# Attention on one core: larger V pieces for pairs 56 and 57, and the last query chunk in six transfers

## The chip, the cores and the metric

The kernel runs on one core of a Trainium2 chip. The metric is device time in microseconds (us); lower is better. The core has TensorE (PE in the profile; its weight loads are PEld), VectorE (DVE), ScalarE (ACT), GpSimd (POOL) and SyncE (SP), and 16 DMA engines that all transfers share.

## What is computed

Grouped-query attention, 16 batches, 32 query heads over 8 key/value heads, 16 queries per head, 2048 keys, head size 128, all in bf16:

```python
B, Hq, Hkv, Sq, Sk, D = 16, 32, 8, 16, 2048, 128

def reference(q, k, v):
    rep = Hq // Hkv
    k = jnp.repeat(k, rep, axis=1)
    v = jnp.repeat(v, rep, axis=1)
    scores = jnp.einsum("bhqd,bhkd->bhqk", q, k) * D ** -0.5
    p = softmax(scores, axis=-1)
    return jnp.einsum("bhqk,bhkd->bhqd", p, v)
```

K and V are 64 MB each; queries and output are 2 MB each.

## The kernel before

**Tiling.** The 4 query heads that share a key/value head have 64 query rows together. The 128 (batch, key/value head) groups are taken two at a time: 64 pairs, numbered 0 to 63 (`NP = 64`). A pair has 1 MB of K and 1 MB of V. Its 128 query rows fill the 128 partitions.

**One pair.** SP loads K (`load_k`, L262) and, six steps later, V (`load_v`, L269). VectorE transposes K in 32x32 blocks (`kt`, L453, L461). TensorE makes the scores (`scores`, L318, L332). VectorE scales them, copies them to `Sneg` and takes the row minimum of the negated scores (L481). GpSimd exchanges the minima between the two halves of the partitions and makes the bias (`exchange`, L193, L208 to L216). ScalarE takes the exponential (`exp`, L520, L529). TensorE transposes the probabilities (`transposes`, L340, L350), ScalarE copies them to `PT` (`evict`, L535, L540), TensorE multiplies with V (`product`, L368), and ScalarE scales by the reciprocal of the row sum (`norm`, L545, L553).

**Two layouts of V.** For pairs below `P4 = NP - 8 = 56` each partition takes one piece of 8 KB of V, which belongs to one of the two groups of the pair; the product is then 64 matmuls, each with 64 rows of contraction (L402). For pairs from P4 on, each partition takes two pieces of 4 KB, one from each group; the product is 32 matmuls with 128 rows of contraction (L391). The layouts of the transposed K (L456), of `Sneg` (L475) and of the exponential's output (L524) follow the same test on P4.

**Queues.** All K, V and all query chunks but one are issued by SP in one order written out by hand (L293): at step t, K of pair t, then a query chunk when t = 4c - 3, then V of pair t - 6. V has four buffers, so its issue waits for the product four pairs earlier (L273); the last four V go to buffers of K (L131) and wait for a transpose of K instead (L271). V of pair 63 comes in two pieces (L284). The outputs of pairs 48 to 62 are held in `Oh` and stored by SP after all loads (L287); the other outputs are stored by ScalarE (L557).

**Queries.** A chunk is the 512 query rows of four pairs (`load_q`, L163): 128 partitions of 1 KB. There are 16 chunks, `NQC = 16`. GpSimd lays a chunk out in `Q4` in two halves (`lay`, L234, L160); before the first half it waits for the chunk's transfer. TensorE transposes them (L365), ScalarE copies them to `QT` (L515) and GpSimd takes each pair's part to `Qs` (L190).

**The end.** The engines run a prologue, a loop of eight steps, and the last pairs written out (`steps`, L120). TensorE's last four steps have an order of their own (L433 to L449): product 56 in `step(NP - 4, 0)`, then scores 62, six idle matmuls that only keep the clock up (`idle`, L409), product 57, scores 63, transposes 61, products 58 and 59, transposes 62, product 60, transposes 63, product 61, five idle matmuls, product 62, three idle matmuls, product 63. The products wait for their V (L371, L373, L389).

Of the kernel before, what the change touches and what calls it, by code (L numbers as in the profile page):

```python
# [16 lines left out]
NQ = 2  # L17
# [8 lines left out]
def bass_standalone__gqa_softmax__sampling_kernel(  # L26
# [18 lines left out]
    G = B * Hkv  # L45
    NP = G // 2
    assert NP % 8 == 0
    P4 = NP - 8
    PH = NP - 1 - sum(HELD)
    NQC = NP // 4  # L50
    scale = float(D) ** -0.5
# [11 lines left out]
    Qn = [sb(f"Qn{i}", [128, 4, 128], BF16) for i in range(NQ)]  # L63
# [24 lines left out]
    sem_q = [sem(f"sem_q{i}") for i in range(NQ)]  # L88
# [20 lines left out]
    qf = q.rearrange("b h s d -> (b h s) d")  # L109
# [6 lines left out]
    LO, HI, LOOP = PVLAG, PH + PVLAG, 8  # L116
    assert (HI - LO) % LOOP == 0 and HI <= P4 - 2


    def steps(eng, step, end):  # L120
        for p in range(LO):
            step(p, p)
        with eng.Fori(LO, HI, LOOP) as base:
            for i in range(LOOP):
                step(base + i, LO + i)
        for p in range(HI, end):
            step(p, p)
# [30 lines left out]
    def spread(eng, c, b):  # L158
        src = Qn[c % NQ][:, :, 64 * b:64 * b + 64]
        return eng.tensor_copy(Q4[:, :, b, :, :], src.unsqueeze(2).to_broadcast([128, 4, 4, 64]))  # L160


    def load_q(eng, c, s):  # L163
        src = qf[bass.ds(512 * c, 512), :].rearrange("(a j) d -> a (j d)", j=4)
        eng.dma_start(Qn[s][:, :, :].rearrange("a j d -> a (j d)"), src).then_inc(sem_q[s], 16)

    lo, hi = slice(0, 64), slice(64, 128)

    with nc.Block() as block:

        @block.gpsimd
        def _(gp):
            gp.memset(warm[:, :], 0.0).then_inc(sem_id, 1)
            gp.iota(iota_t[:, :], [[1, 128]], base=0, channel_multiplier=-1).then_inc(sem_id, 1)
            gp.wait_ge(sem_id, 2)
            gp.tensor_scalar(ident4[:, :], iota_t[:, :], 0.0, None, op0=ALU.is_equal).then_inc(sem_id, 1)


            def held(p):
                if not isinstance(p, int):  # L180
                    gp.nop(nofuse=True)

            def queries(p, i):
                if i % 4 == 0:
                    gp.wait_ge(sem_evq, p + 4)
                if i >= 2:
                    gp.wait_ge(sem_s, p - 1)
                held(p)
                x = i % 4
                gp.tensor_copy(Qs[i % 2][:, :, :], QT[i // 4 % 2][:, :, 128 * x:128 * (x + 1)].bitcast(BF16)).then_inc(sem_qs, 1)  # L190


            def exchange(p, i):  # L193
                known = isinstance(p, int)
                mins, sums = not known or p < NP, not known or p > 0
                x, s, t = slice(0 if mins else 2, 4 if sums else 2), i % NR, (i - 1) % NR
                if mins:
                    gp.wait_ge(sem_max, p + 1)
                if sums:
                    gp.wait_ge(sem_exp, p)  # L200

                gp.wait_ge(sem_qs, min(p + 2, NP) if known else p + 2)
                if known:
                    gp.wait_ge(sem_q4, 2 * laid(p))
                else:
                    gp.wait_ge(sem_q4, p - i + 2 * laid(i))
                held(p)
                gp.tensor_copy(oth[lo, s, x], own[hi, s, x]).then_inc(sem_x[0], 1)  # L208
                gp.wait_ge(sem_x[0], p + 1)
                held(p)  # L210
                gp.tensor_copy(oth[hi, s, x], own[lo, s, x]).then_inc(sem_x[1], 1)  # L211
                gp.wait_ge(sem_x[1], p + 1)
                held(p)
                if mins:
                    for h in range(2):
                        ins = gp.tensor_scalar(nbias[:, s, h:h + 1], own[:, s, h:h + 1], oth[:, s, h:h + 1], None, op0=ALU.min)  # L216
                    ins.then_inc(sem_b, 1)
                if sums:
                    for h, rows in enumerate((lo, hi)):
                        if h:  # L220
                            gp.wait_ge(sem_sum[0], p)
                            held(p)
                        gp.tensor_tensor(  # L223
                            rowsum[rows, t:t + 1], own[rows, s, 2 + h:3 + h], oth[rows, s, 2 + h:3 + h], op=ALU.add,
                        ).then_inc(sem_sum[h], 1)
                    gp.wait_ge(sem_sum[1], p)


            def laid(p):
                c, i = divmod(p, 4)  # L230
                return min(2 + c, NQC) + min(c + (i > 0), NQC - 1)


            def lay(c, b, base=0):  # L234
                if b == 0:
                    gp.wait_ge(sem_q[c % NQ], 2 * base + 16 * (c // NQ + 1))
                    if c:
                        gp.wait_ge(sem_tq, base + 4 * c)
                    held(base)
                spread(gp, c, b).then_inc(sem_q4, 2)  # L240

            def step(p, i):
                known = isinstance(p, int)
                c, base = i // 4, 0 if known else p - i
                exchange(p, i)
                if not known or p + 2 < NP:
                    queries(p + 2, i + 2)
                if i % 4 == 3 and (not known or c + 2 < NQC):
                    lay(c + 2, 0, base)
                if i % 4 == 0 and (not known or c + 1 < NQC):  # L250
                    lay(c + 1, 1, base)

            lay(0, 0)
            for p in range(2):
                queries(p, p)
            lay(1, 0)
            steps(gp, step, NP)
            exchange(NP, NP)

        @block.sync  # L260
        def _(sp):
# [7 lines left out]
            def load_v(p):  # L269
# [5 lines left out]
                done = sem_vx[p - NP + 4] if NP - 4 <= p < NP - 1 else sem_v[p % NV]  # L275
                if p < P4:
                    sp.dma_start(dst, vf[128 * p:128 * (p + 1), :]).then_inc(done, 16)
# [9 lines left out]
            def store_held(p, n):  # L287
                sp.wait_ge(sem_nm, p + n + 1)
                dst = of[128 * p:128 * (p + n), :].rearrange("(x r) d -> r x d", x=n)
                sp.dma_start(dst, Oh[:, p - PH:p - PH + n, :]).then_inc(sem_oh, 16)  # L290

            load_q(sp, 0, 0)
            for t in range(NP + VLAG):  # L293
                if t < NP:
                    load_k(t)
                for c in range(2, NQC):
                    if t == 4 * c - QLEAD:
                        if c == NQ:
                            sp.wait_ge(sem_q4d, 2)
                        sp.wait_ge(sem_q4, max(2, 4 * c - 6))  # L300
                        load_q(sp, c, c % NQ)
                if 0 <= t - VLAG < NP:
                    load_v(t - VLAG)
# [9 lines left out]
        def _(pe):  # L313
# [54 lines left out]
            def product(p, i, out, tail=False, last=False):  # L368
# [13 lines left out]
                pe.nop(nofuse=True)  # L382
                if isinstance(p, int) and p >= P4:
                    pt = PT[i % NPT][:, :, :].bitcast(BF16).rearrange("p (h t) (w q e) -> p h w t e q", h=2, w=2, e=2)
# [67 lines left out]
        def _(dve):  # L452
            def kt(p, i):  # L453
                src = Kn[i % NK][:, :].bitcast(F32)
                dst = KT[i % NKT][:, :]
                if isinstance(p, int) and p >= P4:  # L456

# [11 lines left out]
            def step(p, i):  # L469
# [4 lines left out]
                for h in range(2):  # L474
                    if not known or p < P4:  # L475
                        dst = Sneg[i % 2][:, :].rearrange("p (t h g l e) -> p h g t l e", t=8, h=2, g=2, e=2)[:, h]
# [23 lines left out]
        def _(act):  # L500
# [3 lines left out]
            with act.Fori(1, 2, 1) as c:  # L504
                load_q(act, c, 1)
# [14 lines left out]
            def exp(p, i):  # L520
                act.wait_ge(sem_b, p + 1)
                if i >= 2:
                    act.wait_ge(sem_st[1], p - 1)
                order = "p (h t x) -> p h t x" if isinstance(p, int) and p >= P4 else "p (t h x) -> p h t x"  # L524
                to = P[i % 2][:, :].bitcast(BF16).rearrange(order, x=128, h=2)
# [89 lines left out]
```

## Time and profile before

| | us |
|---|---|
| median of 3 runs (lowest, highest) | 336.94 (336.88, 337.04) |
| the profiled execution | 337.04 |
| its span, first to last instruction | 335.2 |
| busy: DVE, PE, ACT, POOL | 294.9, 279.3, 258.7, 149.4 |
| PE clock granted | 0.99 of full speed |

The core reads 136.31 MB from HBM and writes 2.10 MB, 413 GB/s over the span. The chain of work that ended last, followed back from the last instruction, consists of DMA for 57% of the span, DVE for 16% and PE for 15%. The largest waits of compute engines for data are VectorE's for K (21.7 us in 40 waits) and TensorE's for V (4.0 us in 9 waits that the profile names as such; others are called "issue").

### The profile page before, as it was taken

Reading aid. Unit: us, or ns where it says so; the run is one execution under the profiler, and the core shown is the slowest. Engines: PE = TensorE matmul, PEld = TensorE weight load, DVE = VectorE, ACT = ScalarE, POOL = GpSimd, SP = SyncE. Lnnn points to the kernel's source line nnn. Section 1 sums busy time; section 2 is a strip of 40 time slices with the busy share of each in tenths; the row PEclk is TensorE's granted clock in tenths of the full one; section 3 lists DMA queues with packets and bytes.
Section 4 is the critical chain, followed back from the end, with each engine's and each line's share of the span. In section 5 each row is a group of like instructions: output and inputs, shape, how many; then the busy total and the mean of one; then the engine's idle time right before and its main releaser. Section 6 shows DMA issues by size and latency. Waiting matters only on the chain.

```text
span 335.2 us, 16105 instructions
## 1 busy us (share of the span) xinstructions
PE 279.3 (83%) x6542; PEld 209.0 (62%) x6542; DVE 294.9 (88%) x354; ACT 258.7 (77%) x482; POOL 149.4 (45%) x488
## 2 busy tenths in 40 slices
PE   2557979999998989888897988979879798788786
PEld 1234757777776766666665766757657567567464
DVE  3999998999999989889898898998989989999930
ACT  3286987989897979779688787887878787886873
POOL 4444554363645544444445435354363453543330
PEclk9995999999999999999999999999999999999999
DMA  7999999999999999999999999999999999999998
GB/s 302 429 417 421 414 415 417 422 425 418 425 419 423 421 422 424 419 423 420 421 423 421 421 422 422 421 421 421 421 421 423 420 423 419 422 421 416 412 407 264
DMA packets 31086, 138.60 MB, mean 414 GB/s; under 512 B 11360, under 2 KB 13664, under 8 KB 15712
## 3 DMA queue, kind: packets, MB, share of 16 engines
q1 hardware_dynamic: 23872, 136.68, 98.2%
q10 hardware_dynamic: 7200, 1.74, 2.4%
q8 instruction: 8, 0.13, 0.2%
q14 instruction: 6, 0.05, 0.0%
HBM read 136.31 MB, written 2.10 MB: 413 GB/s over the span
## 4 chain that ended last, share of the span: by engine, by line
DMA 57%; DVE 16%; PE 15%; issue 8%; ACT 2%; POOL 1%; SPq 0%; DVEq 0%; POOLq 0%; ACTq 0%
DMA Vb<-in_v_dram 49%; PE O_ps L402 8%; DVE KT L461 8%; DMA Kn<-in_k_dram 8%; DVE Sneg L481 8%; PE S_ps L332 2%; PE ST_ps L350 2%; ACT P L529 1%; PE ST_ps L412 1%; PE ST_ps L365 1%; POOL nbias L216 0%; PE ST_ps L391 0%; PE S_ps L350 0%; PE O_ps L391 0%; PE S_ps L391 0%
## 5 line engine op out<-in xcount | busy, mean ns | idle before, releaser
L461 DVE STREAM_TRANSPOSE KT<-Kn 128x2048 f32<-128x2048 f32 x64 | 147.7, 2307 | 21.8 <-DMA Kn<-in_k_dram 21.7
L529 ACT ACTIVATE P<-Sneg,nbias 128x1024 bf16<-128x1024 f32 x128 | 145.9, 1142 | 15.3 <-POOL nbias L216 13.4
L481 DVE TENSOR_SCALAR_CACHE_REDUCE Sneg<-S_ps 128x1024 f32<-128x1024 f32 x128 | 149.9, 1205 | 3.3 <-PE S_ps L332 3.2
L402 PE MATMUL O_ps<-Vb,PT 64*64 64x128 bf16 x3584 | 111.1, 216 | 32.1 <-issue 28.1
L402 PEld LDWEIGHTS O_ps<-Vb,PT 64*64 64x64 bf16 x3584 | 102.9, 107 | 51.0 <-issue 51.0
L540 ACT ACTIVATE PT<-ST_ps 128x512 f32<-128x512 f32 x126 | 68.6, 594 | 15.9 <-PE ST_ps L350 15.0
L332 PE MATMUL S_ps<-KT,Qs 32*64 32x512 bf16 x2048 | 74.1, 398 | 6.2 <-DVE Sneg L481 3.9
L350 PE MATMUL ST_ps<-ident,P 128*128 128x128 f32 x504 | 70.0, 283 | 8.2 <-ACT P L529 8.2
L208 POOL COPY oth<-own 64x4 f32<-64x4 f32 (+1 forms) x65 | 11.9, 183 | 137.7 <-DVE Sneg L481 135.6
L350 PEld LDWEIGHTS ST_ps<-ident,P 128*128 128x128 f32 x504 | 54.8, 143 | 16.5 <-ACT P L529 10.7
L332 PEld LDWEIGHTS S_ps<-KT,Qs 32*64 32x64 bf16 x2048 | 27.5, 106 | 31.2 <-issue 17.6
L190 POOL COPY Qs<-QT 128x512 bf16<-128x512 bf16 x64 | 38.9, 609 | 12.1 <-POOL rowsum L223 7.1
L553 ACT ACTIVATE O<-O_ps,rrec 128x128 bf16<-128x128 f32 x48 | 17.5, 364 | 27.6 <-PE O_ps L402 27.5
L216 POOL TENSOR_SCALAR nbias<-own,oth 128x1 f32<-128x1 f32 x128 | 33.9, 280 | 10.6 <-POOL oth L211 9.0
L160 POOL COPY Q<-Qn 128x1024 bf16<-128x1024 bf16 x31 | 32.4, 1044 | 1.3 <-DMA Qn<-in_q_dram 1.3
L223 POOL TENSOR_TENSOR rowsum<-own,oth 64x1 f32<-64x1 f32 x128 | 23.8, 186 | 8.2
L365 PE MATMUL ST_ps<-ident,Q 128*128 128x128 f32 x128 | 22.1, 299 | 4.5 <-POOL Q L160 4.5
L365 PEld LDWEIGHTS ST_ps<-ident,Q 128*128 128x128 f32 x128 | 14.4, 148 | 18.0 <-issue 18.0
L529 ACT ACTIVATION_READ_ACCUMULATOR P<-Sneg,nbias 128x1 f32 x128 | 24.1, 188 | 0.0
L515 ACT ACTIVATE QT<-ST_ps 128x512 f32<-128x512 f32 x32 | 18.4, 576 | 3.7 <-PE ST_ps L365 3.7
L211 POOL COPY oth<-own 64x4 f32<-64x4 f32 (+1 forms) x65 | 11.8, 181 | 7.3
L553 ACT ACTIVATE Oh<-O_ps,rrec 128x128 bf16<-128x128 f32 x12 | 4.4, 367 | 9.7 <-PE O_ps L402 6.7
(30 smaller groups left out, 44.5 us busy)
## 6 DMA issues: line engine op xcount, KB each, us to landing
Kn<-in_k_dram SPq DMA_DIRECT2D x64, 1024.0 KB, 20.5
Vb<-in_v_dram SPq DMA_DIRECT2D x60, 1024.0 KB, 18.4
Kn<-in_v_dram SPq DMA_DIRECT2D x3, 1024.0 KB, 17.4
Qn<-in_q_dram SPq DMA_DIRECT2D x15, 128.0 KB, 20.6
out_dram<-O ACTq DMA_DIRECT2D x49, 32.0 KB, 6.7
Kn<-in_v_dram SPq DMA_DIRECT2D x1, 768.0 KB, 18.2
out_dram<-Oh SPq DMA_DIRECT2D x3, 128.0 KB, 13.8
Kn<-in_v_dram SPq DMA_DIRECT2D x1, 256.0 KB, 16.5
```

The costliest lines, as they stand in the source:

```text
L160: return eng.tensor_copy(Q4[:, :, b, :, :], src.unsqueeze(2).to_broadcast([128, 4, 4, 64]))
L190: gp.tensor_copy(Qs[i % 2][:, :, :], QT[i // 4 % 2][:, :, 128 * x:128 * (x + 1)].bitcast(BF16)).then_inc(sem_qs, 1)
L216: ins = gp.tensor_scalar(nbias[:, s, h:h + 1], own[:, s, h:h + 1], oth[:, s, h:h + 1], None, op0=ALU.min)
L223: gp.tensor_tensor(rowsum[rows, t:t + 1], own[rows, s, 2 + h:3 + h], oth[rows, s, 2 + h:3 + h], op=ALU.add,).then_inc(sem_sum[h], 1)
L332: ins = pe.matmul(S_ps[64 * w:64 * (w + 1), 512 * r:512 * (r + 1)], qs[rows, b, f, 64 * h:64 * (h + 1)], kt[rows, w, b, f], start=(acc == ...
L350: ins = pe.transpose(dst[:, 128 * t:128 * (t + 1)], P[i % 2][:, 128 * x:128 * (x + 1)], ident4[:, :])
L365: ins = pe.transpose(dst[:, 128 * j:128 * (j + 1)], src[:, j, b, :], ident4[:, :])
L402: ins = pe.matmul(out[rows, :], pt[rows, w, t, e, :], vt[rows, x, :], start=(x == 0), stop=(x == 31),)
L461: ins = dve.transpose(dst, src)
L481: ins = dve.tensor_scalar(dst, src, -scale, None, op0=ALU.mult, op1=ALU.min, accum_out=own[:, i % NR, h:h + 1],)
L529: ins = act.activation(to[:, h], of_s[:, h], ACT.Exp, bias=nbias[:, s, h:h + 1], scale=-1.0, accum_out=own[:, t, 2 + h:3 + h],)
L540: act.activation(PT[i % NPT][:, 4 * h:4 * (h + 1), :].rearrange("p t q -> p (t q)"), p_stage_ap(p, h), ACT.Copy,).then_inc(sem_ev[h], 1)
```

## The change

`P4` goes from 56 to 58: V of pairs 56 and 57 comes in 8 KB pieces and their products are of 64 matmuls. The layouts of K, scores and exponentials of these two pairs follow. The last query chunk, number 15, is loaded by six transfers of 112, 8, 4, 2, 1 and 1 partitions, and GpSimd waits for all six; the other chunks are loaded as before.

```diff
-    P4 = NP - 8
+    P4 = NP - 6
...
+    QSPLIT = (112, 8, 4, 2, 1, 1)
+
     def load_q(eng, c, s):
-        src = qf[bass.ds(512 * c, 512), :].rearrange("(a j) d -> a (j d)", j=4)
-        eng.dma_start(Qn[s][:, :, :].rearrange("a j d -> a (j d)"), src).then_inc(sem_q[s], 16)
+        a = 0
+        for n in QSPLIT if isinstance(c, int) and c == NQC - 1 else (128,):
+            src = qf[bass.ds(512 * c + 4 * a, 4 * n), :].rearrange("(a j) d -> a (j d)", j=4)
+            eng.dma_start(Qn[s][a:a + n, :, :].rearrange("a j d -> a (j d)"), src).then_inc(sem_q[s], 16)
+            a += n
...
             def lay(c, b, base=0):
                 if b == 0:
-                    gp.wait_ge(sem_q[c % NQ], 2 * base + 16 * (c // NQ + 1))
+                    more = 16 * (len(QSPLIT) - 1) if isinstance(base, int) and c == NQC - 1 else 0
+                    gp.wait_ge(sem_q[c % NQ], 2 * base + 16 * (c // NQ + 1) + more)
```

## The prediction

> **What bounds the kernel now.** I read the page first: slices, DMA queues, chain of waits. Then the timeline of the last 30 us by engine, then the DMA records of the trace: the size and duration of each packet, and the times at which each transfer's 16 completion marks arrived. The times below that carry no row of their own are such records.
>
> The page, slices and queues:
> ```profile
> DMA  7999999999999999999999999999999999999998
> ...
> q1 hardware_dynamic: 23872, 136.68, 98.2%
> q10 hardware_dynamic: 7200, 1.74, 2.4%
> q8 instruction: 8, 0.13, 0.2%
> ```
> The 16 DMA engines are full from the second slice to the last but one. K and V come at the pace of the packets, and no compute engine is that busy (DVE 88%). So a saving inside the stream moves the end only if the compute that follows the last transfers can start earlier too. That is read from TensorE's rows of the tail, as start, duration, line, count and wait before:
> ```profile
> 311.84 1.08 PE L391 MATMUL O_ps<-Vb,PT 128*64 128x128 bf16 x32 [0.98 <-issue]
> 312.85 1.09 PE L350 MATMUL ST_ps<-ident,P 128*128 128x128 f32 x8
> 313.97 1.11 PE L332 MATMUL S_ps<-KT,Qs 32*64 32x512 bf16 x32
> 315.01 1.47 PE L412 MATMUL ST_ps<-ident 128*128 128x512 bf16 x6
> 316.90 1.08 PE L391 MATMUL O_ps<-Vb,PT 128*64 128x128 bf16 x32 [0.42 <-issue]
> 319.01 1.11 PE L332 MATMUL S_ps<-KT,Qs 32*64 32x512 bf16 x32 [1.02 <-DVE Sneg L481]
> ...
> 327.25 1.09 PE L391 MATMUL S_ps<-Kn,PT 128*64 128x128 bf16 x32
> 328.26 1.25 PE L412 MATMUL ST_ps<-ident 128*128 128x512 bf16 x5
> 329.79 1.08 PE L391 MATMUL O_ps<-Kn,PT 128*64 128x128 bf16 x32 [0.27 <-issue]
> 330.81 0.82 PE L412 MATMUL ST_ps<-ident 128*128 128x512 bf16 x3
> 331.67 1.10 PE L391 MATMUL ST_ps<-Kn,PT 128*64 128x128 bf16 x32
> ```
> Against the landings: V56 lands at 311.75 and its product starts at 311.84; V57 at 316.81 and 316.90; V62 at 329.70 and 329.79; the first piece of V63 at 331.63 and 331.67. The four waits called "issue" or shown as nothing are waits for V. Behind the last product come one normalisation (332.81) and one store, 2.4 us. So the landing of V63 sets the end, and the compute chain from K63 runs close behind: without V62's landing, product 62 could start 0.27 us earlier.
>
> **The change part by part.**
>
> Pieces. V56 and V57 go from 256 packets of 4 KB to 128 of 8 KB each. In the records a 4 KB packet takes 163.7 ns and an 8 KB packet 311.5 ns, so a pair saves 2 x 163.7 - 311.5 = 15.9 ns on each of 8 packets of an engine, 0.127 us, and 0.25 us for two. The landings say less: from V55 (306.72) over K62, V56, K63 to V57 (316.81) four transfers take 10.09 us; the four before, from K60 (299.26) to K62 (309.22), all of 8 KB, take 9.96. That is 0.13 us for two. I take 0.13, because a landing is what the product waits for, and keep 0.25 as the other end. All V after them, 58 to 63, come earlier by that.
>
> Products 56 and 57. A product of 64 matmuls takes 1.98 us (next work 1.90 after its start) where one of 32 takes 1.08 (next work 1.01):
> ```profile
> 306.81 1.98 PE L402 MATMUL O_ps<-Vb,PT 64*64 64x128 bf16 x64 [0.92 <-issue]
> ```
> So each costs TensorE 0.90 us more, 1.80 in all, in the tail where the order is fixed. What hides it: behind product 56 follow transposes 60, scores 62 and the six idle matmuls; they slip 0.84 (0.90 less the 0.06 by which V56 is early), and the wait of 0.42 before product 57 takes half. Product 57 then starts at 317.32 at the latest and scores 63 at 317.32 + 1.90 = 319.22, where now it waits 1.02 us for the minimum of pair 62 and starts at 319.01. What is late next is at most 0.21: DVE's two passes over scores 63, GpSimd's minimum, ScalarE's exponential, transposes 63, product 61, and then the 0.27 before product 62 takes it up. ScalarE's copy of transposes 60 ends near 315.4, so exponential 61 slips from 314.97 to there, with 1.62 us of waiting behind it before exponential 62. Cost: nothing; without the two waits of 0.42 and 1.02 it would be 1.80 - 0.27 = 1.5 us. Scores 62 slip to about 314.7 and end at 315.8, before DVE is free for them at 316.52. The layouts of K, scores and exponentials change with the pieces, but K's transpose is 2.31 us and a score pass 1.18 to 1.22 us on either side of pair 56.
>
> Queries. Chunk 15 is issued after K57; five more issues of 0.43 us on SP, about 2.4 us with gaps:
> ```profile
> 263.99 0.43 SPq L165 DMA_DIRECT2D Qn<-in_q_dram  x1
> 268.55 0.33 SPq L277 DMA_DIRECT2D Vb<-in_v_dram  x1
> ```
> SP then waits until 268.55 for product 47, so 4.13 us cover it, and V51 and K58 behind go out when they did; the queue ahead is 18 us deep, so not even a late issue would leave the engines idle. Its reader is GpSimd:
> ```profile
> 285.75 1.04 POOL L160 COPY Q<-Qn 128x1024 bf16<-128x1024 bf16 x1
> 288.68 0.18 POOL L208 COPY oth<-own 64x4 f32<-64x4 f32 x1 [1.89 <-DVE Sneg L481]
> ```
> The chunk lands at 284.35, 1.40 before the copy, and 1.89 of waiting follows it: 3.3 us of cover. In the stream the trace shows no transfer of fewer than 128 rows (96 KB of output still has 128). Bounds: the same 128 packets of 1 KB (46 ns), and 5 x 16 completion packets of 9 ns more, spread evenly: 0.045 us. At the other end the 16 rows of the small transfers go to one engine, which then carries 23 rows for 8: 15 x 46 + 5 x 9 = 0.74 us on that engine, and the others gain one row, -0.05. I take the even end, +0.05, as the only q rows that I have are even. [...] No row here shows which engines are late.
>
> Sum: -0.13 + 0.05 + 0 = -0.08 us, on a profiled execution of 337.04 us (span 335.2 and 1.8 around it), so 336.96. The median shown, 336.94, lies 0.10 below the profiled one: 336.86.
>
> **The rivals.**
>
> R1, the full packet saving and one row less on the late engines: -0.25 - 0.05 = -0.30, 336.64. For it: the engines are full, so packet time is stream time. Against: the landings of V56 and V57 show half of it. The compute chain allows it only while scores 63 slip little.
>
> R2, crowded engine: the small q transfers fall on one engine that is already the latest. Then V63 lands at -0.13 + 0.74 = +0.61, 337.55. For it: the 16 marks of a transfer are 1.8 to 1.9 us apart at the end, ten engines late together within 0.75 us, six early. Against: an early engine takes 0.74 without harm, as the gap is more than 1 us.
>
> R3, slower: instruction fetches. Eight 16 KB packets of q8, each about 1.07 us of one engine; after each, one engine goes from the early group to the late for good. Three fall in the tail, at 317.58, 324.72 and 330.99, some 250 TensorE instructions apart. The third comes when the early engines have finished, and costs nothing. The change adds 128 TensorE instructions there, so the fetch moves forward to about 328, before V63 is in. It decides if it hits an engine with less than 1.07 us of lead: then V63 lands up to 1.07 later, -0.08 + 1.07 = +0.99, 337.93. Against: the fetches seen so far each hit an early engine.
>
> R4, small transfers in sequence: each extra one pays its own time to landing, 2.3 us by the one q transfer that met idle engines; 5 x 2.3 = 11.5, less the 3.3 of cover, +8.2, 345.1. Against: transfers overlap in the queue; K and V land every 2.5 us though each takes 20. [...]
>
> **How the numbers follow.** Forecast 0.46, R1 0.16, R2 0.10, R3 0.18, R4 0.02; 0.08 stay for a gain over 0.2% (a later engine relieved, which I can't derive). 0.2% is 0.67 us, about what a measurement of this kernel can tell from no change. The forecast, R1 and R2 are all within it, 0.72 less 0.02 for what lies at their edges: same 0.70; faster 0.09; slower 0.21 (R3, R4, and a crowded engine above 0.67). Range 336.5 to 337.9: below it a gain past R1, above it R3 at full size and R4. The forecast's own range is 336.7 to 337.1.
>
> **What would show it.** Product groups of 64 at L402 up to pair 57, 1.98 us each; V56 and V57 landing 0.06 and 0.13 earlier; scores 63 no later than 319.2, with little or no wait before it; products 62 and 63 still starting within 0.1 us of their V. I am wrong if scores 63 slip by more than 0.3 us (cover mis-sized), if the spread of V63's marks passes 2.2 us (R2, R3; the place of the late q8 packet tells which), or if GpSimd's copy of chunk 15 waits (R4).

## The result and the profile after

The changed kernel takes 338.03 us (median of 8 runs, 337.91 to 338.38); the kernel before, beside it, 337.02. The ratio is 1.0030, interval 1.0021 to 1.0040: slower by 1.0 us, where -0.08 was forecast and the range ended at 337.9. The profiled execution took 338.02 us with a span of 336.1. Each ratio is the one on record, with its 95% interval; it is not the quotient of the medians.

The page of the changed kernel, the lines that answer to those shown of before:
```profile
DMA  7999999999999999999999999999999999999997
...
q1 hardware_dynamic: 23632, 136.68, 98.0%
q10 hardware_dynamic: 7200, 1.74, 2.3%
q8 instruction: 8, 0.13, 0.2%
```
The queue of K, V and queries has 240 packets fewer: 256 fewer of V and 16 more completion marks. The engines are as full as before; only the last slice is emptier, because the end now waits for something else.

TensorE's timeline of the tail in the changed kernel (start, duration, engine and line, count, wait before; products of 64 are L408 here, those of 32 L397, scores L338):
```profile
312.13 1.98 PE L408 MATMUL O_ps<-Vb,PT 64*64 64x128 bf16 x64 [0.91 <-issue]
...
317.50 1.98 PE L408 MATMUL O_ps<-Vb,PT 64*64 64x128 bf16 x64
319.41 1.26 PE L338 MATMUL S_ps<-KT,Qs 32*64 32x512 bf16 x32
...
324.86 0.55 PE L397 MATMUL S_ps<-Kn,PT 128*64 128x128 bf16 x13 [0.23 <-issue]
326.20 0.75 PE L397 MATMUL S_ps<-Kn,PT 128*64 128x128 bf16 x19 [0.79 <-issue]
...
327.90 1.09 PE L397 MATMUL S_ps<-Kn,PT 128*64 128x128 bf16 x32
...
330.10 1.08 PE L397 MATMUL O_ps<-Kn,PT 128*64 128x128 bf16 x32
...
331.87 0.91 PE L397 MATMUL ST_ps<-Kn,PT 128*64 128x128 bf16 x25
333.37 0.38 PE L397 MATMUL ST_ps<-Kn,PT 128*64 128x128 bf16 x7 [0.58 <-issue]
```
Two products are torn, that is, TensorE stops inside a run of equal matmuls. Product 60 stops after 13 of its 32 matmuls for 0.79 us, product 63 after 25 for 0.58 us, by the modelled end of a matmul; from start to start the second gap is 0.80. No wait of the program stands there: product 60 has none inside, and the second piece of V63 had landed at 332.47, and the 25th matmul, which waits for it, started at 332.56. The profile calls both "issue": TensorE waited for nothing that it shows.

What it does show is the instruction queue. In the packet records a 16 KB packet of q8 starts at 323.77 and one at 330.96, and TensorE goes on 2.43 and 2.41 us after these starts. In every product torn in the traces of this case, TensorE goes on 2.2 to 2.6 us after the start of such a packet. Before the change the three packets of the tail started at 317.58, 324.72 and 330.99, and no product was torn.

From the first tear to the second, TensorE's records number 256: 124 matmuls, 125 weight loads and 7 semaphore waits. By the same count, less the 128 instructions of the change, the kernel before passes such a place, the end of a block of 256, inside product 58, at about 321.7, and does not stop: the last packet had started 4.1 us earlier. In the changed kernel the packets start 1.4 and 1.6 us before TensorE reaches the two ends. So a block end alone tears nothing here; it did with a packet 1.4 and 1.6 us before it, not with one 4.1 us before. That the limit lies near 2.4 us is an estimate from the 2.2 to 2.6 us above. Why the packets start when they do, no run here shows.

SP and GpSimd around query chunk 15 in the changed kernel:
```profile
263.95 2.02 SPq L169 DMA_DIRECT2D Qn<-in_q_dram  x6
268.51 0.36 SPq L283 DMA_DIRECT2D Vb<-in_v_dram  x1
```
```profile
285.71 1.04 POOL L160 COPY Q<-Qn 128x1024 bf16<-128x1024 bf16 x1
289.01 0.18 POOL L213 COPY oth<-own 64x4 f32<-64x4 f32 x1 [2.27 <-DVE Sneg L487]
```
Both covers held. But behind chunk 15 every transfer lands later: K56, ahead of it, lands at 278.96 (before 279.01), V51, right behind it, at 287.19 (286.83), V55 at 307.08 (306.72). The whole stream has lost 0.41 us there. V56 and V57 give back 0.14, and V63 lands at 332.47, 0.16 later than before.

The last matmul starts at 333.53, before at 332.55: 0.98 us. Without the tear product 63 would have needed 1.10 from 331.87, to 332.97, where it ended at 332.77 before. So 0.20 is the later start, which goes with the late stream, and 0.78 the tear. Product 60's tear does not reach product 63's start: product 61 starts 0.65 later, 62 only 0.31 and 63 0.20, as the waits for V take the rest.

### The profile page after: what moved, and what is told of

The parts are those of the page before. It is cut to its first block, busy times and chain, and to the rows that moved or that the text cites. A ratio compares the mean times of both kernels' runs of the same rounds, so it can differ in the third digit from the quotient of the medians.

```text
span 336.1 us, 16238 instructions
## 1 busy us (share of the span) xinstructions
PE 282.1 (84%) x6606; PEld 211.5 (63%) x6606; DVE 294.8 (88%) x354; ACT 258.6 (77%) x482; POOL 149.4 (44%) x488
## 3 DMA queue, kind: packets, MB, share of 16 engines
q10 hardware_dynamic: 7200, 1.74, 2.3%
## 4 chain that ended last, share of the span: by engine, by line
DMA 51%; PE 25%; DVE 14%; issue 7%; ACT 2%; POOL 1%; SPq 0%; DVEq 0%; POOLq 0%
DMA Vb<-in_v_dram 49%; PE O_ps L408 11%; DVE KT L467 7%; DVE Sneg L487 7%; PE ST_ps L356 5%; PE S_ps L338 5%; DMA Kn<-in_k_dram 2%; ACT P L535 2%; PE ST_ps L418 1%; PE ST_ps L371 1%; PE S_ps L397 1%; PE ST_ps L397 1%; PE O_ps L397 1%; POOL nbias L221 0%; PE S_ps L356 0%
## 5 line engine op out<-in xcount | busy, mean ns | idle before, releaser
L408 PE MATMUL O_ps<-Vb,PT 64*64 64x128 bf16 x3712 | 115.0, 216 | 32.2 <-issue 28.3
L408 PEld LDWEIGHTS O_ps<-Vb,PT 64*64 64x64 bf16 x3712 | 106.5, 107 | 52.0 <-issue 52.0
L338 PE MATMUL S_ps<-KT,Qs 32*64 32x512 bf16 x2048 | 74.5, 400 | 5.5 <-DVE Sneg L487 3.2
L338 PEld LDWEIGHTS S_ps<-KT,Qs 32*64 32x64 bf16 x2048 | 27.4, 106 | 30.4 <-issue 16.4
L371 PE MATMUL ST_ps<-ident,Q 128*128 128x128 f32 x128 | 22.8, 307 | 4.5 <-POOL Q L160 4.5
```

The lines of the kernel that those rows point to most:

```text
L338: ins = pe.matmul(S_ps[64 * w:64 * (w + 1), 512 * r:512 * (r + 1)], qs[rows, b, f, 64 * h:64 * (h + 1)], kt[rows, w, b, f], start=(acc == ...
L371: ins = pe.transpose(dst[:, 128 * j:128 * (j + 1)], src[:, j, b, :], ident4[:, :])
L408: ins = pe.matmul(out[rows, :], pt[rows, w, t, e, :], vt[rows, x, :], start=(x == 0), stop=(x == 31),)
```

## The experiments

Code theory, read from the 16 KB packets of q8 and the 256 records between the two tears: TensorE's instructions come in blocks of 256; where a block ends and the next has not come, it stands still (0.79 and 0.58 us here); 128 added instructions moved two block ends into products 60 and 63. Stream theory: the split of the queries delays K and V, and this is the whole loss. In each batch the kernel before ran beside the others; its medians were 337.09, 337.01 and 337.17.

**The two parts alone.**

```diff
 p4_only
-    P4 = NP - 8
+    P4 = NP - 6
```


> P4 = NP - 6 alone, query chunk 15 in one transfer. Code theory (TensorE's instructions arrive in blocks of 256; the 128 added ones move two block ends into products 60 and 63, where TensorE stands still for 0.8 and 0.6 us): both breaks stay, V lands about 0.15 us earlier than before and 0.35 earlier than with the whole change; about 337.7 us, +0.5 to +0.8 against before. Stream theory (the split of the queries delays K and V, and this delay is the whole loss): faster than before by 0.15, about 336.9, and no break in products 60 and 63.

Measured 337.68 (before 337.09), ratio 1.0013, interval 1.0005 to 1.0022. Both tears are there, in the same places, products 60 (13 and 19 matmuls) and 63 (25 and 7). V57 lands 0.07 earlier than before, V63 0.15. So V comes earlier and the kernel is slower: the stream theory falls as the whole account.
```profile
324.47 0.55 PE L391 MATMUL S_ps<-Kn,PT 128*64 128x128 bf16 x13 [0.26 <-issue]
325.75 0.75 PE L391 MATMUL S_ps<-Kn,PT 128*64 128x128 bf16 x19 [0.73 <-issue]
...
333.03 0.38 PE L391 MATMUL ST_ps<-Kn,PT 128*64 128x128 bf16 x7 [0.58 <-issue]
```

```diff
 q_only
+    QSPLIT = (112, 8, 4, 2, 1, 1)
```


> The six query transfers alone, P4 = NP - 8. Code theory: no break in the last products; the stream is 0.3 to 0.35 us later from chunk 15 on, V63 with it; about 337.35, +0.3. Stream theory: V63 as late and the whole loss of 1.0 us, 338.0. If the split costs nothing: 337.0.

Measured 337.68, ratio 1.0019, interval 1.0011 to 1.0028, twice the 0.3 expected. No tear. The step of the stream at chunk 15 is 0.39 us in the profiled execution (K56 0.34, V51 0.73 later than before). The 0.34 was there before the split: K12, at 53.6 us, is already 0.39 late, so executions differ from their first 60 us on, and a profile shows one of them. The two parts give 0.59 each, 1.18 together; that differs from the 1.0 of the change by less than their intervals are wide.

**Moving the block ends.** By the code theory, 128 instructions in TensorE's prologue shift every later block end by 128 instructions; they leave pieces and queries alone.

```diff
 after_pad128, before_pad128 (PAD = 128)
             for i in range(4):
+                for _ in range(2 * PAD // 4):
+                    pe.wait_ge(sem_id, 3)
                 step(0, i)
```


> The kernel before, with the same 128 waits in TensorE's prologue and nothing else: pieces and queries as before. Code theory: the block ends now fall into products 60 and 63 as in the changed kernel, both show a break of 0.6 to 0.8 us, and the time is 337.6 to 337.9, +0.6 to +0.9. Stream theory: 337.0, no break.

> The whole change, with 128 waits that are already met added to TensorE's prologue, 32 before each of its first four steps, so that all later block ends fall on the same instructions of the tail as before the change. Code theory: products 60 and 63 run through, 337.2 (+0.2 against before, what the stream is late). Stream theory: no effect, 338.0. If the added waits delay the start themselves: later than 338.0.

The 256 waits make 128 instructions more on the page (16233, before 16105). The times are of no use: 340.48 for before_pad128 (ratio 1.0103, 1.0076 to 1.0129) and 341.10 for after_pad128 (1.0121, 1.0106 to 1.0136). Each added instruction took 106 ns, TensorE came late in the first steps, and the DMA rate fell to 332 to 374 GB/s in two slices. The places answer, though. TensorE in before_pad128, whose pieces and queries are those of before (products of 32 are L392):
```profile
327.56 0.55 PE L392 MATMUL S_ps<-Kn,PT 128*64 128x128 bf16 x13 [0.41 <-issue]
328.71 0.75 PE L392 MATMUL S_ps<-Kn,PT 128*64 128x128 bf16 x19 [0.60 <-issue]
...
334.62 0.93 PE L392 MATMUL ST_ps<-Kn,PT 128*64 128x128 bf16 x25
336.12 0.38 PE L392 MATMUL ST_ps<-Kn,PT 128*64 128x128 bf16 x7 [0.57 <-issue]
```
Products 60 and 63 are torn at the 13th and the 25th matmul, to the matmul where the changed kernel is. In after_pad128 they run through, and product 58 is torn (23 and 9).

To free the times of the slow start, the 128 instructions were made of 64 matmuls, each with a weight load, behind scores 0, whose result is not used:

```diff
 before_mm128, after_mm128
             scores(0, 0, first=True)
+            x = ident4[:, :].bitcast(BF16)
+            for i in range(PAD // 2):
+                h = i % 2
+                pe.matmul(O_ps[64 * h:64 * (h + 1), 0:128], x[:, 0:64], x[:, 0:128], start=True, stop=True)
```


> The kernel before with 64 matmuls (128 TensorE instructions, result not used) behind scores 0, where TensorE waits some 3 us; the 128 waits of the earlier try took 106 ns each and cost the start 3 us, these should take 2 to 4 us in all and cost it nothing. Pieces and queries as before. Code theory: breaks in product 60 after its 13th and in product 63 after its 25th matmul, 337.6 to 337.8 (+0.6 to +0.8). Stream theory: 337.0, no break.

> The whole change with the same 64 matmuls behind scores 0: 256 instructions more than before, a whole block, so the block ends of the tail fall where they fell before the change. Code theory: no break in products 60 and 63, perhaps one in product 58 as with the 128 waits, which V60 and later hide; 337.2 to 337.5 (what is left is the late stream). Stream theory: 338.0.

before_mm128: 337.84 (337.69 to 338.2) beside 337.17; ratio 1.0012, interval 0.9996 to 1.0029, which just holds 1; the medians differ by the 0.67 expected. TensorE's tail:
```profile
325.03 0.55 PE L392 MATMUL S_ps<-Kn,PT 128*64 128x128 bf16 x13 [0.36 <-issue]
326.12 0.75 PE L392 MATMUL S_ps<-Kn,PT 128*64 128x128 bf16 x19 [0.54 <-issue]
...
332.05 0.94 PE L392 MATMUL ST_ps<-Kn,PT 128*64 128x128 bf16 x25
333.56 0.38 PE L392 MATMUL ST_ps<-Kn,PT 128*64 128x128 bf16 x7 [0.57 <-issue]
```
The tears of the change, without the change.

after_mm128: 338.02, ratio 1.0017, interval 1.0000 to 1.0034, where 337.2 to 337.5 was expected. A miss on the time, not on the place:
```profile
321.76 0.86 PE L398 MATMUL O_ps<-Vb,PT 128*64 128x128 bf16 x23
323.45 0.44 PE L398 MATMUL O_ps<-Vb,PT 128*64 128x128 bf16 x9 [0.83 <-issue]
...
332.03 1.09 PE L398 MATMUL ST_ps<-Kn,PT 128*64 128x128 bf16 x32
```
Products 60 and 63 run through, and the last matmul starts 0.64 earlier than in the changed kernel. But the last store ends late: 15 of its 16 completion marks come within 0.17 us, where in the other runs all 16 come within 0.18, and the last one 0.45 later, at 335.47. So most of the 0.64 went to the store. A ninth 16 KB packet starts at 333.26 in this run, but it ends before the store's first data packet starts at 334.41; that it delays this one mark is not shown. The stream is also later here: its step from K56 to V51 is 0.60 us.

**Fewer idle matmuls.** The other way to move the block ends: leave out instructions ahead of product 63.

```diff
 p4_idle042 (from p4_only), before_idle042, after_idle042
-IDLE = (6, 5, 3)
+IDLE = (0, 4, 2)
```


> P4 = NP - 6, one query transfer, and IDLE = (0, 4, 2) for (6, 5, 3): eight idle matmuls, 16 TensorE instructions, fewer ahead of product 63. Code theory: the last block end moves 16 instructions later, past the last matmul of product 63, and the one in product 60 from after its 13th matmul to after its 21st; product 63 runs through, V lands 0.15 us earlier than before: 336.9, a gain of 0.1 to 0.2 against before. If the breaks have nothing to do with the instructions' places: a break in product 63 after its 25th matmul as in p4_only, 337.6.

> The kernel before with IDLE = (0, 4, 2) alone, the control for the run with both: TensorE waits for V in these places anyway, so 337.0 to 337.1. If fewer idle matmuls slow the clock of TensorE in the tail: later by 0.2 us or more, and a matmul of the tail longer than 216 to 219 ns.

> The whole change with IDLE = (0, 4, 2). Code theory: product 63 runs through, the stream stays 0.15 to 0.25 us later than before; 337.2 to 337.4. Stream theory: 338.0. Break in product 60, if any, after its 19th matmul, since six of the eight idle matmuls precede it.

p4_idle042 takes 336.86, 0.82 less than p4_only (beside 337.01 and 337.09 for the kernel before). Its TensorE:
```profile
324.46 0.72 PE L391 MATMUL S_ps<-Kn,PT 128*64 128x128 bf16 x19 [0.21 <-issue]
325.60 0.58 PE L391 MATMUL S_ps<-Kn,PT 128*64 128x128 bf16 x13 [0.42 <-issue]
...
331.45 1.10 PE L391 MATMUL ST_ps<-Kn,PT 128*64 128x128 bf16 x32 [0.26 <-DMA Kn<-in_v_dram]
```
Product 63 is whole and waits for V again, and the tear in product 60 has moved by six matmuls, from the 13th to the 19th: six idle matmuls precede product 60. (The 21st that was expected counted all eight.) The block end that tore product 63 falls past its last matmul, as eight matmuls fewer precede it. Against the kernel before the median is 0.15 lower, but the ratio is 1.0008, interval 0.9983 to 1.0034, as two of the twelve runs took 338.63 and 341.46: a gain over it is not shown.

before_idle042 takes 337.16, ratio 1.0006, interval 0.9992 to 1.0020: leaving out idle matmuls gains nothing by itself. after_idle042 takes 337.55, ratio 1.0002, interval 0.9984 to 1.0019; the median is 0.48 below that of the change and 0.38 above before. Product 63 is whole and waits for V63, which lands 0.74 later than before the change in the profiled execution; 0.57 of that was there at K56, ahead of the split.

**What the split costs.** Three other splits of chunk 15, with P4 = NP - 8. What is expected of engines and their rows is an estimate from the completion packets: q1 has 2368 of them for 148 transfers before, 16 each, and 16 more after the change. No record shows which engine takes a row.

```diff
 q_112_16; q_64_64
-    QSPLIT = (112, 8, 4, 2, 1, 1)
+    QSPLIT = (112, 16)
...
+    QSPLIT = (64, 64)
 q_columns
+        src = qf[bass.ds(512 * c, 512), :].rearrange("(a j) d -> a (j d)", j=4)
+        n = 512 // len(QSPLIT) if isinstance(c, int) and c == NQC - 1 else 512
+        for x in range(0, 512, n):
+            eng.dma_start(Qn[s][:, :, :].rearrange("a j d -> a (j d)")[:, x:x + n], src[:, x:x + n]).then_inc(sem_q[s], 16)
```


> P4 = NP - 8; the last query chunk in two transfers of all 128 rows, each with half of every row (512 B), so rows go to the engines as in any other transfer. If the cost of the split is that rows go to other engines than in all other transfers: no slowing of the 8 KB packets beside it (313 to 320 ns on the mean of that stretch) and V51 less than 0.1 us later; 337.1. If any further transfer costs it: 8 KB packets at 350 ns and more, V51 0.3 to 0.4 later, 337.4 to 337.7.

> P4 = NP - 8; the last query chunk in two transfers of 112 and 16 rows, both on 16 engines, no transfer of fewer. If it is the rows on other engines (seven rows for each engine, not eight): 8 KB packets slowed to 350 ns as with six transfers, V51 0.3 to 0.4 us later, 337.4 to 337.7. If it is the four transfers on fewer than 16 engines: no slowing, V51 less than 0.1 later, 337.1.

> P4 = NP - 8; the last query chunk in two transfers of 64 rows, four rows for each of 16 engines in both. If the cost is that rows go to other engines than in a transfer of 128 rows: 8 KB packets at 350 ns and more beside it and V51 0.3 to 0.5 us later, 337.4 to 337.7. If it is a row count that leaves engines unequal (112 and 16, 8, 4, 2, 1): none of it, 337.1.

q_columns: 337.08, ratio 1.0000, interval 0.9988 to 1.0012. q_112_16: 337.63, ratio 1.0020, 1.0005 to 1.0035. q_64_64: 337.77 beside 337.17, ratio 1.0012, 0.9995 to 1.0030. The same 4 us of the profile, in which chunk 15 comes in, for before, the change, q_columns and q_64_64 (us, busy of each engine with its instructions, clock, DMA share, GB/s):
```profile
281.50:285.50 4.00, 3.92 (x104) 3.12 (x104) 3.65 (x6) 2.74 (x6) 1.52 (x7) 1.00 1.03 418
```
```profile
281.50:285.50 4.00, 3.97 (x104) 3.10 (x104) 3.28 (x6) 2.75 (x6) 1.56 (x7) 1.00 1.03 369
```
```profile
281.50:285.50 4.00, 3.87 (x104) 3.12 (x104) 3.65 (x6) 2.74 (x6) 1.46 (x7) 1.00 1.02 404
```
```profile
281.50:285.50 4.00, 3.78 (x104) 3.11 (x104) 3.05 (x6) 2.74 (x7) 1.38 (x7) 1.00 1.02 340
```
The DMA share is the same, the rate is not: each packet takes longer. An 8 KB packet of these 4 us takes 316, 359, 319 and 386 ns on the mean (364 in q_112_16). The step of the stream from K56 to V51, against the kernel before, is 0.41 us in the change, 0.07 in q_columns, 0.49 in q_112_16 and 0.68 in q_64_64. The same six transfers as in the change give 0.38 to 0.68 in five traces, and the five traces of other kernels with one transfer 0.02 at most. So the split costs, but which of the three splits across rows costs most is not shown. Neither the number of transfers nor those with few marks make it: two transfers of 64 rows, each with 16 marks, have the cost, and two of 128 short rows next to none. What the slow splits share is transfers of other than 128 rows.

Why packets take longer beside such transfers, 359 to 386 ns for 316, is not shown.

## Why the prediction was wrong

- **What bounds the kernel: right for before.** After it, V63 no longer sets the end; the tear in product 63 does.
- **Pieces, -0.13: right.** p4_only gains 0.12 from K62 to V57 (0.05 late to 0.07 early), the change 0.14. The landings were the better row than the packets' 0.25.
- **Products, "Cost: nothing": the step that failed.** The cover was sized well: scores 63 start at 319.10 in p4_only (319.22 at the latest was said), with no wait before it. In the change they start at 319.41, 0.40 later than before and past the 0.3 that was to show a mis-sized cover; they are 0.31 behind p4_only, where V56 lands 0.29 earlier, so this is the late stream. But the 128 instructions were costed by their run time alone. They also move the block ends of TensorE's code, and that costs 0.78 us in product 63; the sum had no term for it.
- **R3 saw the fetch and priced the wrong victim.** It had the packets, their distance of about 250 instructions, and nearly the size of the loss, +0.99; the size is luck, as it comes from another mechanism. It put a packet at about 328, where none starts (323.77 and 330.96), and let it delay one DMA engine and so V63. V63's marks are 1.74 us apart at the end (1.89 before), so no engine fell further behind; the loss is TensorE standing still, in product 63 until 2.41 us after the start of a packet. From tear to tear it is 256 records in p4_only, before_pad128 and before_mm128 too, and the tears last 0.42 to 0.83 us on the matmul rows shown.
- **Queries, +0.05: the size was off.** It measured 0.41. The nearest row, a q transfer of 128 rows, was the wrong one, and the high end of 0.74 stood on one crowded engine (R2), while here all 16 marks of V51 come later than before, by 0.3 to 0.8 us. There are 16 completion packets more, not the 80 of the even end: 32 for the six transfers, which 16 + 8 + 4 + 2 + 1 + 1 would give. So the small transfers do not have 16 each; on how many engines they run is an estimate from that number.
- **SP and GpSimd's covers: right.** Six issues took 2.02 us of the 4.13, and chunk 15 was never waited for. R4 did not happen.
- **R1** could not: it needed the split to be free.

## What to carry to other kernels

Where a long tail is written out, count TensorE's instructions: added ones can cost more by where the code's block ends fall (0.78 us in product 63 here) than by their own time, and a group of equal instructions torn without a wait is the sign of it. Moving the last end past the last product, by leaving out filler, took 0.82 us off here (p4_idle042 against p4_only). The kernel before has an end inside a product too and loses nothing by it, so look at how long before the end its packet starts (4.1 us there, 1.4 and 1.6 in the changed kernel). In this full stream, splitting a transfer along the row moved it by 0.07 us and splitting it across partitions by 0.41 to 0.68.

## What else the runs showed

Idle matmuls do keep the clock in this tail. In before_idle042 TensorE waited 1.94 us for V57 without them (us, PE busy, clock, DMA share, GB/s):
```profile
316.00:319.20 3.20, 1.74 (x40) 0.73 1.03 406
319.20:321.20 2.00, 2.00 (x34) 0.58 1.01 406
```
The granted clock was 0.73 and 0.58 in the two stretches, where it is 1.00 in both in the kernel before with its idle matmuls, and scores 63 took 1.92 us, not 1.11. The end hid it, as V63 came later still. In p4_idle042, where the same wait was 1.05 us, the clock stayed at 1.00.
